# Masked attention and a two-layer MLP on one core: second-layer weights split ahead into DRAM, x work of GpSimd in halves, another order of the block products

## The chip, the cores and the metric

The kernel runs on one core of a Trainium2 chip. The metric is the device time of one execution in microseconds; less is better. A core has TensorE (PE, matrix products into PSUM), VectorE (DVE), ScalarE (ACT), GpSimd (POOL) and SyncE (SP, which here issues all the DMAs). Each engine works through its own queue in order; semaphores tie the queues together.

## The reference

Everything is float32, except that the weights come as 64-bit floats.

```python
scores = scale * q @ k.T                                  # 8 batches x 8 heads, 576 x 64
scores = where(scores >= max(scores) - tau, scores, -1e9)
attn = softmax(scores)
x = (attn @ v) arranged as (8 * 576, 8 * 64)              # 4608 tokens x 512
h = x @ w_in                                              # 512 -> 2048
g = maximum(h, 0) + alpha * minimum(h, 0)
out = g @ w_out                                           # 2048 -> 512
```

To keep float32's precision at a faster matmul, an operand is split in two parts of the type fp32r: hi is a rounded copy (always ACT, `split_hi`), lo is the original less hi (DVE or POOL, `split_lo`). A product then takes three matmuls: hi by hi, hi by lo, lo by hi.

## The kernel before

**Attention.** 32 pairs of heads, nine steps ("cycles") each, 288 in all. In cycle i DVE masks unit i, PE makes the scores of unit i+2 and turns unit i, and ACT makes the exponentials. What a pair needs behind its last unit (its products with v, the reciprocals, a trip of them through DRAM, three operations on POOL, the write of x to DRAM as `xs`) is queued some nine to seventeen cycles behind the pair's first unit. Into the gaps `Mlp.cycle` (line 759) puts work of the MLP for the first 6 of the 16 blocks of 128 hidden units: first-layer steps (`step_l1`, 12 matmuls for 256 tokens) and second-layer steps (`step_l2`). Tokens go in 18 groups of 256, and a group is ready when its batch's attention is done: groups 13 and 14 from cycle 265, and 15 to 17 only behind the last pair.

**Bridge.** What is left of these 18 groups becomes `jobs` (line 1028): for each, x is fetched (`fetch_x`), the first layer is made for six blocks, and the second layer of the job before (`second_layer`, 36 matmuls) stands behind the first of them. Beside it the first-layer weights of the other ten blocks are read from DRAM, where they were put, decoded, during the attention (`wid`); the seven sums that the next stage needs are made and split (`sums_at`) into the tiles `wa`.

**Stage A.** The remaining ten hidden blocks use a block scheme with seven products in place of eight (Winograd's form of Strassen's). Tokens go in six x blocks of 768; with the five pairs of hidden blocks that gives 30 units. `x_at` loads an x block, makes four sums (`sub7`, `add6`, `sub4`, `sub5`) and splits seven operands (hi on ACT, lo on POOL). `product_a` makes one product, six matmuls of 384 columns, per cycle. Products 1, 6, 5 and 3 of a unit add up in one PSUM bank X, 7 and 4 in W, 2 in Y; between two of a bank `after_a`, one cycle behind each product, reads the bank (ACT copies it to `c`, or DVE adds to it), and the bank's next product waits for that. `ORDER` is the order in which the products of neighbouring units follow each other. The results go to DRAM as `gd`. Meanwhile the second layer's weights are decoded from their 64-bit form, a block of 128 at a time, in steps on ACT, POOL and DVE (`word_at`: size, clamp, shift, sign, power, rest, done, a cycle apart) into the tile `wo32`. In the last five units `weights_b` makes the seven sums of each pair from it and splits them into the places of the first-layer weights as these fall free.

**Stage B.** The second layer of the ten blocks in the same scheme, nine units of seven products, 30 matmuls each. `gates_at` loads `gd` (as `gr`) and splits; `after_b` adds to the earlier partial sums (`pin`) and writes the output.

**What sets the order.** `at_cycle(c, fn)` puts a function into cycle c; all cycles are emitted in order, so PE, ACT, DVE and POOL run their instructions in this order, each as early as its data and its queue allow. The DMAs on SP are put in order by the framework.

Of the kernel before, what the change touches and what calls it, by code (L numbers as in the profile page):

```python
# [21 lines left out]
P = 128  # L22
# [3 lines left out]
F1 = 6  # L26
# [10 lines left out]
GB = 11  # L37
ENG1 = ('vpp', 'vpp')
# [42 lines left out]
def tile_masked_attention_moe(  # L81
# [606 lines left out]
    class Mlp:  # L688
# [70 lines left out]
        def cycle(self, i, used, slot):  # L759

            self.room = min(self.room, TH3) + CYCLE - used
            l1 = False
            if self.l1 and i >= self.gap and self.live < GB:
                if self.l1[0][2] is None:
                    self.step_l1(i)
                elif slot and self.room > TH1 and ("i", fcs1[self.l1[0][2]]) in ready:
                    l1 = True
                    self.room -= 1.31
            while self.l2 and self.l2[0][0] <= i and self.l2[0][4] in self.l2[0][2]["g"] and ("o", fcs1[self.l2[0][4]]) in ready and self.room > TH2:
                self.step_l2(i)  # L770
                self.room -= 0.216
            return l1
# [48 lines left out]
    ORDER = ((0, 1), (1, 5), (0, 7), (0, 2), (1, 3), (0, 6), (0, 4))  # L821
# [17 lines left out]
    def word_at(c, w, load, done, fc=None):  # L839


        def rest():
            low = f(w.low)
            w.eng[1].tensor_tensor(low, low, f(w.high), op=ALU.mult)

        at_cycle(load, w.load)
        at_cycle(c, w.size, *(() if fc is None else (tiny_sb[:, fc : fc + 1],)))
        at_cycle(c + 1, w.clamp)
        at_cycle(c + 2, w.shift)
        at_cycle(c + 3, w.sign)  # L850
        at_cycle(c + 4, w.power)
        at_cycle(c + 5, rest)
        at_cycle(c + 6, done, w)
# [48 lines left out]
    with tc.manual_schedule(engines=ENGINES) if ENGINES else ExitStack():  # L902
# [57 lines left out]
        left = [ExitStack() for _ in range(6)]  # L960
# [87 lines left out]
        first_weights(i + 4, 6)  # L1048
# [12 lines left out]
        def first_layer(job, j):  # L1061
            fc = fcs1[j]
            name = f"{job.name}_{fc}"
            while "x" not in job.x:
                cycle()
            ph = ps_2.tile([P, 512], F32, tag="ph", name=f"ph{name}", bufs=4)
            layer1_into(ph, fc, job.n, job.x["x"])
            cycle()
            t = prelu(mem.mp1, G1, fc, job.n, ph, name, 2)
            job.g[j] = mem.mp1.tile([P, 2, G1], F32R, tag="g", name=f"g{name}", bufs=GB)  # L1070
            split_g(job.g[j], t, job.n)
# [23 lines left out]
        for num, job in enumerate(jobs):  # L1095
            fetch(num + 1)
            for k, j in enumerate(job.todo):
# [7 lines left out]

        puts = second_layer(pending, mem.ws)
        left[2].close()
        p1.close()
        mem.xr = pool(2, "xraw", "left")
        mem.br = pool(3, "br", "right")  # L1110
        mem.pa = pool(4, "pa", "right")

        start = {}
        steps = []
        c = i + 1
        for n in range(NA + NB + 1):
            for lag, prod in {NA: TURN, NA + NB - 1: LAST, NA + NB: ()}.get(n, ORDER):
                u = n - lag
                if 0 <= u < NA + NB:
                    start[u, prod] = c  # L1120
                    steps.append((u, prod))
                    c += 1 if u < NA else 3
        begin = start[0, 1]
        end = c
        place = {step: n for n, step in enumerate(step for step in steps if step[0] >= NA)}
# [3 lines left out]
        def x_at(s):  # L1129
            u = s * NP  # L1130
            st = {}
            need = {n: start[u, n] for n in USE}
            first = s == 0

# [12 lines left out]
            tt = (nc.vector if first else nc.gpsimd).tensor_tensor  # L1147
# [20 lines left out]
            def hi(n):  # L1168
                slot = (7 * s + USE.index(n) - 7 * (NA // NP - 1)) % XB
                home = mem.pa if slot < 7 else mem.xr  # L1170
# [5 lines left out]
            def lo(n):  # L1176
                split_lo(nc.vector if first and n in (7, 6) else nc.gpsimd, xop[s, n][1], st[src(n)], xop[s, n][0])

            if first:
                at = lambda c, fn, *a: fn(*a)  # L1180
            else:
                at = at_cycle
            at(need[1] - 32, load)
            for m, n in enumerate(USE):
                c = need[1] - 22 + 3 * m
                if not first and m >= XB - 7:
                    c = max(c, start[u - 1, USE[m + 7 - XB]] + 2)
                fn = {7: sub7, 6: add6, 4: sub4, 5: sub5}.get(n)
                if fn:
                    at(c - 1, fn)  # L1190
                at(c, hi, n)
                at(c + 1, lo, n)

        x_at(0)
        for put in puts:
            put()
        left[5].close()
# [66 lines left out]
        wo32 = mem.br.tile([P, NP, 2, DM], F32, name="wo32")  # L1264
        def late_word(n, c):
            fc = fcs2[n]
            w = Split64(mem.ws, ("w0", 3), mem.ws, ("w1", 2), "ppp", *src_o(fc))

            def done(w):
                dst = wo32[:, n // 2, n % 2]  # L1270
                nc.vector.scalar_tensor_tensor(
                    dst, f(w.t), turn_sb[:, fc : fc + 1], f(w.low), op0=ALU.mult, op1=ALU.add
                )

            word_at(c, w, c - 4, done, fc)

        for n in range(NJ):
            late_word(n, begin + 8 + 14 * n)
# [3 lines left out]
        def weights_b(pr):  # L1282
            m = DM // 2
            u = NA - NP + pr
            blk = lambda j, k: wo32[:, pr, j, k * m : (k + 1) * m]
            st = {1: blk(0, 0), 2: blk(1, 0), 3: blk(1, 1), 5: blk(0, 1), 6: blk(0, 0), 4: blk(1, 0)}
            tt = nc.vector.tensor_tensor

            def sub7():
                st[7] = mem.br.tile([P, m], F32, tag="wt", name=f"wt{pr}", bufs=2)  # L1290
                tt(st[7], st[3], st[5], op=ALU.subtract)

            def sub5():
                tt(st[5], st[5], st[1], op=ALU.subtract)

            def add6():
                tt(st[6], st[7], st[1], op=ALU.add)

            def sub4():
                tt(st[4], st[2], st[6], op=ALU.subtract)  # L1300

            def hi(n):
                bsum[pr, n] = mem.wa.tile([P, 2, m], F32R, tag=f"wa{pr}_{n}", name=f"wb{pr}_{n}")
                split_hi(bsum[pr, n][:, 0], st[n])

            def lo(n):
                split_lo(nc.vector if n in (1, 2, 5) else nc.gpsimd, bsum[pr, n][:, 1], st[n], bsum[pr, n][:, 0])

            for n in USE:
                c = start[u, n] + 2  # L1310
                if n == 7:
                    at_cycle(c - 1, sub7)
                    at_cycle(c - 1, sub5)
                fn = {6: add6, 4: sub4}.get(n)
                if fn:
                    at_cycle(c, fn)
                at_cycle(c, hi, n)
                at_cycle(c + 1, lo, n)

        def gates_at(s):  # L1320
# [57 lines left out]
            for n in USE:  # L1378
# [4 lines left out]
                if fn:  # L1383
                    at_cycle(c - 2, fn)
# [32 lines left out]
        def turn_over():  # L1417
            left[2].close()
# [80 lines left out]
```

## Time and profile before

| | us |
|---|---|
| median of 3 runs | 1441.19 (1441.01 to 1441.2) |
| the profiled execution | 1439.3 |
| its span, from the first to the last instruction | 1437.5 |
| PE busy in the span | 1323.2 (92%) |
| DVE busy | 1143.2 (80%) |
| ACT busy | 971.8 (68%) |
| POOL busy | 745.6 (52%) |

The profile is of one execution. Its times count from the span's start. A row of a timeline has start, duration, engine, line, operation, out<-in, a count, and in brackets how long the engine sat idle before and who ended that. A group of instructions has its count, busy time and mean in ns, and the idle time before them. Matmuls are pipelined: two overlap, so their starts and not their durations give the pace, and a busy PE can still run at a lower granted clock.

### The profile page before, as it was taken

What the parts mean: (1) busy time and instruction counts of PE and PEld (TensorE: products, weight loads), DVE (VectorE), ACT (ScalarE), POOL (GpSimd) and SP (SyncE); (2) the same over time, 40 slices, a digit from 0 to 9 for tenths busy, and PEclk for the clock granted to TensorE, in tenths of its full rate; (3) what the DMA queues carried; (4) which work ended last, traced back from release to release, by engine and by line L of the source; (5) the groups of instructions that cost most, each with busy time, mean ns of one, the idle gap of its engine ahead of it and who ended that gap; (6) DMA issues with size and microseconds to landing.
All of it is one profiled execution on the core that took longest, in us unless ns stands there. A gap on an engine that the chain in (4) does not pass through costs nothing.

```text
span 1437.5 us, 26187 instructions
## 1 busy us (share of the span) xinstructions
PE 1323.2 (92%) x8998; PEld 1229.8 (86%) x8998; DVE 1143.2 (80%) x2122; ACT 971.8 (68%) x2109; POOL 745.6 (52%) x875
## 2 busy tenths in 40 slices
PE   5998999999899898999999998879888898999998
PEld 4666889989889898898889987778788898999998
DVE  7998988988978988888888855756666568878886
ACT  7887888888878887888888844356555565333332
POOL 4874765774765766666666646555465542000000
PEclk9999999999999999999999999989999999999999
DMA  7646455555545455455544314345452365656541
GB/s 227 187 115 171 126 138 143 156 151 145 157 127 146 138 150 149 132 158 146 144 136 131 85 48 156 103 146 157 154 161 94 127 202 174 195 180 205 190 144 59
DMA packets 146165, 210.31 MB, mean 146 GB/s; under 512 B 16016, under 2 KB 89008, under 8 KB 146032
## 3 DMA queue, kind: packets, MB, share of 16 engines
q1 hardware_dynamic: 146032, 208.63, 49.4%
q8 instruction: 72, 1.18, 0.3%
q14 instruction: 61, 0.50, 0.1%
HBM read 111.75 MB, written 54.67 MB: 116 GB/s over the span
## 4 chain that ended last, share of the span: by engine, by line
PE 59%; issue 11%; DVE 11%; ACT 8%; POOL 7%; DMA 3%; SPq 1%; POOLq 0%; DVEq 0%; ACTq 0%
PE av L577 10%; PE pX L1396 9%; PE s L430 9%; PE acca L253 7%; PE t L474 5%; PE pha L217 5%; PE pW L1396 4%; PE pX L1219 4%; PE pY L1396 2%; DVE p L465 2%; DVE nmx L445 2%; PE pW L1219 1%; POOL xl L869 1%; ACT p L453 1%; DVE eo L530 1%
## 5 line engine op out<-in xcount | busy, mean ns | idle before, releaser
L445 DVE TENSOR_REDUCE nmx<-s 128x1 f32<-128x576 f32 x288 | 216.7, 752 | 64.6 <-PE s L430 61.2
L465 DVE SCALAR_TENSOR_TENSOR p<-s,thr,p 128x576 f32<-128x576 f32 x256 | 206.8, 808 | 3.2 <-ACT thr L458 2.7
L453 ACT ACTIVATE p<-s,nmx 128x576 f32<-128x576 f32 x256 | 190.3, 743 | 8.8 <-DVE nmx L445 8.4
L430 PE MATMUL s<-kh,qst 128*128 128x288 f32 x640 | 144.9, 316 | 49.2 <-DVE p L465 31.7
L1219 PE MATMUL pX<-xh,wa 128*128 128x384 f32 x480 | 142.5, 355 | 43.3 <-DVE pZ L1259 25.4
L253 PE MATMUL acca<-wo,ga 128*128 128x512 f32 x540 | 168.8, 425 | 1.5 <-POOL ga L247 1.5
L430 PEld LDWEIGHTS s<-kh,qst 128*128 128x128 f32 x640 | 100.2, 192 | 79.4 <-issue 39.6
L474 PE MATMUL t<-ident,p 128*128 128x128 f32 x1024 | 156.5, 276 | 0.0
L217 PE MATMUL pha<-xh,wi 128*128 128x256 f32 x720 | 146.9, 287 | 6.1 <-ACT pra L230 4.6
L1219 PEld LDWEIGHTS pX<-xh,wa 128*128 128x128 f32 x480 | 92.7, 198 | 50.2 <-DVE pZ L1259 28.9
L430 PE MATMUL s<-kl,qst 128*128 128x288 f32 x640 | 133.9, 299 | 0.0
L1396 PE MATMUL pX<-wb,gh 128*128 128x256 f32 x720 | 130.2, 283 | 0.0
L217 PEld LDWEIGHTS pha<-xh,wi 128*128 128x128 f32 x720 | 117.4, 190 | 13.1 <-ACT pra L230 7.7
L474 PEld LDWEIGHTS t<-ident,p 128*128 128x128 f32 x1024 | 127.7, 143 | 0.2
L866 ACT ACTIVATE gh<-gr 128x1280 fp32r<-128x1280 f32 x45 | 57.4, 1276 | 88.2 <-PE pX L1396 39.2
L1396 PEld LDWEIGHTS pX<-wb,gh 128*128 128x128 f32 x720 | 112.2, 191 | 0.0
L577 PE MATMUL av<-eo,vst 128*128 128x322 f32 (+1 forms) x512 | 107.7, 334 | 0.2 <-ACT xb L590 0.2
L253 PEld LDWEIGHTS acca<-wo,ga 128*128 128x128 f32 x540 | 95.7, 194 | 14.0 <-POOL ga L247 1.9
L530 DVE TENSOR_TENSOR eo<-t,eo 128x512 fp32r<-128x512 f32 (+1 forms) x168 | 97.3, 592 | 9.8 <-ACT eo L526 9.3
L430 PEld LDWEIGHTS s<-kl,qst 128*128 128x128 f32 x640 | 102.6, 192 | 0.0
L1396 PE MATMUL pX<-wb,gl 128*128 128x256 f32 x360 | 101.7, 283 | 0.0
L217 PE MATMUL pha<-xl,wi 128*128 128x256 f32 x360 | 101.4, 282 | 0.0
(207 smaller groups left out, 3824.5 us busy)
## 6 DMA issues: line engine op xcount, KB each, us to landing
gd<-c SPq DMA_DIRECT2D x90, 192.0 KB
gr<-gd SPq DMA_DIRECT2D x24, 640.0 KB
kr<-in_k_dram SPq DMA_DIRECT2D x31, 320.0 KB
rb<-rvd SPq DMA_DIRECT2D x64, 144.0 KB
xs<-xa SPq DMA_DIRECT2D x32, 288.0 KB
pin<-part SPq DMA_DIRECT2D x18, 512.0 KB
out_dram<-pin SPq DMA_DIRECT2D x18, 512.0 KB
vr<-in_v_dram SPq DMA_DIRECT2D x28, 320.0 KB
```

The source lines that it names most:

```text
L217: nc.tensor.matmul(ph[:, :n], w[:, c, :], xx[:, c, :n], start=(c == 0 and ti == 0), stop=(c == NCC - 1 and ti == 2),)
L253: nc.tensor.matmul(acc[:m, :], gg[:, g, o : o + m], w, start=(first and ti == 0), stop=(last and ti == 2))
L430: nc.tensor.matmul(ps[:, h, :288], w, kk[:, a + h * 288 : a + (h + 1) * 288], start=(ki == 0 and i == 0), stop=(ki == 1 and i == n - 1),)
L445: nc.vector.tensor_reduce(self.nmx[:, j : j + 1], self.S[u][0][:, :, :288], axis=AX.XY, op=ALU.max, negate=True)
L453: nc.scalar.activation(pj, ps[:, :, :288], AF.Exp, bias=nmx[:, j : j + 1], scale=1.0)
L465: nc.vector.scalar_tensor_tensor(pj, ps[:, :, :288], thr[:, j : j + 1], pj, op0=ALU.is_ge, op1=ALU.mult, accum_out=self.sm[:, c : c + 1])
L474: nc.tensor.transpose(tb[:, c, :], pt[:, j, j * D + c * P : j * D + (c + 1) * P], ident)
L530: nc.vector.tensor_tensor(dst[1], ps, f(dst[0]), op=ALU.subtract)
L577: nc.tensor.matmul(pa[:m, :n], w, x, start=(part == 0 and c == 0), stop=(part == z.parts[-1] and c == NKC))
L866: nc.scalar.activation(dst, src, AF.Copy)
L1219: nc.tensor.matmul(ph[:, :H1], a, x[:, c], start=(fresh and c == 0 and ti == 0), stop=(c == 1 and ti == 2), skip_group_check=not fresh,)
L1396: nc.tensor.matmul(acc[:, tb * H2 : (tb + 1) * H2], g[:, pr, tb * P : (tb + 1) * P], w, start=(fresh and n == 0 and ti == 0), stop=(n == l ...
```

## The change

It has these parts. The diff has line numbers of the kernel before.

1. `HOLD = 14`: `Mlp.cycle` issues no first-layer step from cycle 274 on.
2. `ORDER` swaps its fifth and sixth entries: product 6 comes before the earlier unit's product 3.
3. `word_at` gets a pace. The second layer's words use `LATE`: size at 0, clamp 1, shift 3, sign 4, power 5, rest 6, done 9.
4. `late_pair` takes the place of `late_word` and `weights_b`: two words are decoded 12 cycles apart, their sums made, all seven split (lo always on POOL) and written to DRAM (`wod`), a pair every 28 cycles. `weights_b` only reads them back, two cycles behind the last use of the place.
5. From the second x block on, `x_at`'s sums and lo parts go to POOL as two instructions of 128x384 in place of one of 128x768.
6. The first x block is loaded, and its first operand made, ahead of the last two second layers of the bridge, which now follow each other; the rest of its operands comes behind them. For that three places of operands lie in a pool of their own (`xe`), and the last job's sixth g has a place in `ws`.
7. The first weights are 9 cycles apart in place of 6, and the gates' `sub3` has another cycle.

```diff
+HOLD = 14
...
-                elif slot and self.room > TH1 and ("i", fcs1[self.l1[0][2]]) in ready:
+                elif slot and i < total - HOLD and self.room > TH1 and ("i", fcs1[self.l1[0][2]]) in ready:
...
-    ORDER = ((0, 1), (1, 5), (0, 7), (0, 2), (1, 3), (0, 6), (0, 4))
+    ORDER = ((0, 1), (1, 5), (0, 7), (0, 2), (0, 6), (1, 3), (0, 4))
...
+    EARLY, LATE = (0, 1, 2, 3, 4, 5, 6), (0, 1, 3, 4, 5, 6, 9)
...
+        for d, step in zip(pace[1:], (w.clamp, w.shift, w.sign, w.power, rest)):
+            at_cycle(c + d, step)
+        at_cycle(c + pace[6], done, w)
...
-        first_weights(i + 4, 6)
+        first_weights(i + 4, 9)
...
             for k, j in enumerate(job.todo):
                 first_layer(job, j)
-                if k == 0 and pending:
+                if k == 0 and pending and not last:
                     second_layer(pending, mem.mp1)
-            pending = job
-        puts = second_layer(pending, mem.ws)
+            if not last:
+                pending = job
...
+            def tt(out, a, b, op):
+                if first:
+                    nc.vector.tensor_tensor(out, a, b, op=op)
+                else:
+                    for c in range(2):
+                        nc.gpsimd.tensor_tensor(out[:, c], a[:, c], b[:, c], op=op)
...
+            def lo(n):
+                xh, xl = xop[s, n]
+                if first and n in (7, 6, 2):
+                    split_lo(nc.vector, xl, st[src(n)], xh)
+                else:
+                    for c in range(2):
+                        split_lo(nc.gpsimd, xl[:, c], st[src(n)][:, c], xh[:, c])
+
+            if first:
+                for fn in (load, sub7):
+                    fn()
+                hi(1)
+                lo(1)
+                add6()
+                sub5()
+
+                def others():
+                    for n in USE[1:]:
+                        if n == 4:
+                            sub4()
+                        hi(n)
+                        lo(n)
+
+                return others
...
         left[2].close()
+        mem.xr = pool(2, "xraw", "left")
+        others = x_at(0)
+        second_layer(pending, mem.mp1)
+        puts = second_layer(jobs[-1], mem.ws)
         p1.close()
-        mem.xr = pool(2, "xraw", "left")
+        mem.xe = pool(6, "xe", "left")
         mem.br = pool(3, "br", "right")
         mem.pa = pool(4, "pa", "right")
+        others()
+        for put in puts:
+            put()
...
+        H = DM // 2
+        wod = [dram.tile([len(USE), P, 2, H], F32, name=f"wod{pr}") for pr in range(NP)]
+
+        def late_pair(pr, c):
+            st = {}
+
+            def done(r, w):
+                if r == 0:
+                    st["w"] = mem.br.tile([P, 2, DM], F32, tag="wq", name=f"wq{pr}", bufs=2)
+                fc = fcs2[2 * pr + r]
                 nc.vector.scalar_tensor_tensor(
-                    dst, f(w.t), turn_sb[:, fc : fc + 1], f(w.low), op0=ALU.mult, op1=ALU.add
+                    st["w"][:, r], f(w.t), turn_sb[:, fc : fc + 1], f(w.low), op0=ALU.mult, op1=ALU.add
                 )
...
+            def hi(n):
+                st["hl", n] = mem.br.tile([P, 2, H], F32R, tag="wb", name=f"wb{pr}_{n}", bufs=2)
+                split_hi(st["hl", n][:, 0], st[n])
+
+            def lo(n):
+                t = st["hl", n]
+                split_lo(nc.gpsimd, t[:, 1], st[n], t[:, 0])
+                nc.sync.dma_start(wod[pr][USE.index(n)], f(t))
+
+            for r in range(2):
+                fc = fcs2[2 * pr + r]
+                w = Split64(mem.ws, ("w0", 3), mem.ws, ("w1", 2), "ppp", *src_o(fc))
+                word_at(c + 12 * r, w, c + 12 * r - 8, lambda w, r=r: done(r, w), fc, LATE)
+            at_cycle(c + 24, sums)
+            for k, n in enumerate(USE):
+                at_cycle(c + 26 + 2 * k, hi, n)
+                at_cycle(c + 27 + 2 * k, lo, n)
+
+        for pr in range(NP):
+            late_pair(pr, begin + 8 + 28 * pr)
...
-            for n in USE:
-                c = start[u, n] + 2
...
+            def load(n):
+                bsum[pr, n] = mem.wa.tile([P, 2, H], F32R, tag=f"wa{pr}_{n}", name=f"wb{pr}_{n}")
+                nc.sync.dma_start(f(bsum[pr, n]), wod[pr][USE.index(n)])
+
+            for n in USE:
+                at_cycle(start[NA - NP + pr, n] + 2, load, n)
...
-                    at_cycle(c - 2, fn)
+                    at_cycle(max(need[6], need[2]) - 4 if n == 3 else c - 2, fn)
```

More of the change, by code (lines that the diff above doesn't have):

```diff
@@ L837, in tile_masked_attention_moe, with word_at @@
     wid = [dram.tile([P, DM], F32, name=f"wid{fc}") for fc in fcs2]
-    def word_at(c, w, load, done, fc=None):
+    EARLY, LATE = (0, 1, 2, 3, 4, 5, 6), (0, 1, 3, 4, 5, 6, 9)
+    def word_at(c, w, load, done, fc=None, pace=EARLY):
         def rest():
@@ L959, in tile_masked_attention_moe @@
         at.close()
-        left = [ExitStack() for _ in range(6)]
+        left = [ExitStack() for _ in range(7)]
         pool = lambda k, name, side: left[k].enter_context(tc.tile_pool(name=name, bufs=1, side=side, reuse_waits="tile"))
@@ L1096, in tile_masked_attention_moe @@
             fetch(num + 1)
+            last = num == len(jobs) - 1
             for k, j in enumerate(job.todo):
                 first_layer(job, j)
-                if k == 0 and pending:
+                if k == 0 and pending and not last:
                     second_layer(pending, mem.mp1)
-            pending = job
-        puts = second_layer(pending, mem.ws)
-        left[2].close()
-        p1.close()
-        mem.xr = pool(2, "xraw", "left")
[L1110 to L1125, printed above, removed]
+            if not last:
+                pending = job
         xop = {}
@@ L1131, in x_at @@
             st = {}
-            need = {n: start[u, n] for n in USE}
             first = s == 0
+            need = None if first else {n: start[u, n] for n in USE}
             def load():
@@ L1189, in x_at @@
                 if fn:
[L1190 to L1194, printed above, removed]
+                    at_cycle(c - 1, fn)
+                at_cycle(c, hi, n)
+                at_cycle(c + 1, lo, n)
+        left[2].close()
+        mem.xr = pool(2, "xraw", "left")
+        others = x_at(0)
+        second_layer(pending, mem.mp1)
+        puts = second_layer(jobs[-1], mem.ws)
+        p1.close()
+        mem.xe = pool(6, "xe", "left")
+        mem.br = pool(3, "br", "right")
+        mem.pa = pool(4, "pa", "right")
+        others()
         for put in puts:
             put()
+        start = {}
+        steps = []
+        c = i + 1
+        for n in range(NA + NB + 1):
+            for lag, prod in {NA: TURN, NA + NB - 1: LAST, NA + NB: ()}.get(n, ORDER):
+                u = n - lag
+                if 0 <= u < NA + NB:
+                    start[u, prod] = c
+                    steps.append((u, prod))
+                    c += 1 if u < NA else 3
+        begin = start[0, 1]
+        end = c
+        place = {step: n for n, step in enumerate(step for step in steps if step[0] >= NA)}
         left[5].close()
@@ L1271, in done, with sums @@
                 nc.vector.scalar_tensor_tensor(
-                    dst, f(w.t), turn_sb[:, fc : fc + 1], f(w.low), op0=ALU.mult, op1=ALU.add
+                    st["w"][:, r], f(w.t), turn_sb[:, fc : fc + 1], f(w.low), op0=ALU.mult, op1=ALU.add
                 )
-            word_at(c, w, c - 4, done, fc)
-        for n in range(NJ):
-            late_word(n, begin + 8 + 14 * n)
+            def sums():
+                blk = lambda j, k: st["w"][:, j, k * H : (k + 1) * H]
+                st.update({1: blk(0, 0), 2: blk(1, 0), 3: blk(1, 1), 5: blk(0, 1)})
+                for n in (7, 6, 4):
+                    st[n] = mem.br.tile([P, H], F32, tag=f"sumo{n}", name=f"sumo{n}_{pr}")
+                tt = nc.vector.tensor_tensor
+                tt(st[7], st[3], st[5], op=ALU.subtract)
+                tt(st[6], st[7], st[1], op=ALU.add)
+                tt(st[5], st[5], st[1], op=ALU.subtract)
+                tt(st[4], st[2], st[6], op=ALU.subtract)
@@ L1287, in weights_b @@
[L1287 to L1304, printed above, removed]
@@ L1417, in turn_over @@
         def turn_over():
+            left[6].close()
             left[2].close()
```

42 lines of the change are left out of this document (7 added, 35 removed).

## The prediction, made before the changed kernel had run

> **What bounds the kernel now.** I cut the span at the stages that the code has and read the windows view first. Columns: TensorE busy (instructions), its weight loads, DVE, ACT, POOL, then granted clock, DMA share and GB/s.
>
> ```profile
> 806.00:840.00 34.00, 34.00 (x251) 32.50 (x250) 30.15 (x68) 27.27 (x69) 18.27 (x23) 1.00 0.12 43
> 840.00:868.50 28.50, 25.78 (x152) 22.10 (x150) 7.48 (x17) 8.47 (x21) 11.69 (x17) 1.00 0.23 72
> 868.50:928.00 59.50, 54.05 (x325) 48.24 (x326) 39.12 (x73) 26.59 (x71) 40.89 (x51) 0.94 0.43 141
> 928.00:1206.00 278.00, 234.66 (x1256) 227.49 (x1255) 178.71 (x288) 156.71 (x304) 141.27 (x97) 0.95 0.44 143
> 1206.00:1437.50 231.50, 227.09 (x1897) 226.88 (x1895) 182.81 (x164) 79.90 (x67) 2.82 (x2) 0.99 0.53 169
> ```
>
> From 1206.0 (stage B, second layer) TensorE never waits and the change leaves its 1,890 matmuls alone: nothing to win there. From 928 to 1206 (stage A, first layer, 30 units of seven products) 43 us are idle. The same view for line 1219 alone, one row for each x block of five units, and last a stretch without a stall:
>
> ```profile
> 928.00:976.30 48.30, 38.02 (x198) 37.07 (x198) 0.89 0.42 135
> 976.30:1023.30 47.00, 40.15 (x212) 39.10 (x211) 0.93 0.44 140
> 1023.30:1069.10 45.80, 38.85 (x212) 37.90 (x211) 0.96 0.50 156
> 1069.10:1115.70 46.60, 39.87 (x211) 38.80 (x211) 0.93 0.36 119
> 1115.70:1157.50 41.80, 37.37 (x212) 36.41 (x211) 1.00 0.37 124
> 1157.50:1206.00 48.50, 40.39 (x217) 37.88 (x216) 0.98 0.55 179
> 1126.70:1144.40 17.70, 17.70 (x104) 17.70 (x103) 1.00 0.32 111
> ```
>
> The last row holds 17 products of six matmuls: 1.041 us each. Five units, 35 products, would take 36.4 us; the blocks take 41.8 to 47.0. The first row (33 products, 34.4 us) is 13.9 long, the next four together 35.6, the last (36 products to the first of stage B, 37.5 us) 11.0: **60.5 us lost in stage A**. The granted clock of 0.89 to 0.96 in the long rows is part of it: behind a long gap the matmuls run slower for a few us.
>
> Who ends the waits (waits view, 928 to 1206; us in total, times, longest):
>
> ```profile
> PE pX L1219 <- DVE pZ L1259: 25.4, 10, 5.4
> PE pX L1219 <- ACT c L1236: 17.9, 10, 6.4
> POOL xl L869 <- ACT xh L866: 76.7, 27, 12.3
> ```
>
> Products 1, 6, 5, 3 of a unit add into one bank X, and each must wait until ACT or DVE has read the one before. Those two are not full; they are held up. The timelines of the longest stall and of one that comes with every x block:
>
> ```profile
> 1001.58 2.03 POOL L1161 TENSOR_TENSOR xt<-xt,xr 128x768 f32<-128x768 f32 x1
> 1001.94 2.22 DVE L152 SCALAR_TENSOR_TENSOR wto<-wro,wto 128x512 int32<-128x512 int32 x1
> 1006.71 2.27 DVE L1271 SCALAR_TENSOR_TENSOR wo<-wto,turn_sb,wro 128x512 f32<-128x512 f32 x1 [0.62 <-POOL wro L844]
> 1010.10 0.69 PE L1219 MATMUL pX<-xh,wa 128*128 128x384 f32 x1 [5.42 <-DVE pZ L1259]
> 1022.72 1.58 ACT L866 ACTIVATE xh<-xr 128x768 fp32r<-128x768 f32 x2 [1.71 <-POOL xr L1158]
> 1025.67 0.44 PE L1219 MATMUL pX<-xh,wa 128*128 128x384 f32 x1 [1.14 <-ACT c L1236]
> ```
>
> A decode step on DVE that reads and writes SBUF stands still until GpSimd's whole x operation is over (2.22 and 2.27 us); the `done` step also waits for GpSimd's multiply. Behind them in DVE's queue is pZ, and TensorE loses 5.42. In the second kind ACT's hi copy waits for a GpSimd subtraction, and the copy that frees the bank is queued behind it.
>
> By the Trainium skill ("SBUF — State Buffer", Who interferes with whom) the shared port pair is an exclusive lock held for the whole instruction. The two DVE rows agree; by that rule an x operation cut in two bounds such a wait by its half.
>
> **The change part by part.** *Halves, equal gaps, later decode steps, weights ahead.* GpSimd's durations:
>
> ```profile
> L77 POOL TENSOR_TENSOR kl<-kr,kh 128x320 fp32r<-128x320 f32 x8 | 7.0, 894 | 21.4 <-ACT kh L357 21.4
> L1158 POOL TENSOR_TENSOR xr<-xr,xr 128x768 f32<-128x768 f32 x5 | 9.2, 1844 | 0.0
> L869 POOL TENSOR_TENSOR wb<-wo,wb 128x256 fp32r<-128x256 f32 x15 | 13.7, 913 | 20.5 <-ACT wb L866 17.6 <-PE pW L1219 2.9
> L844 POOL TENSOR_TENSOR wro<-wro 128x512 f32<-128x512 f32 x10 | 10.4, 1040 | 19.4 <-DVE wro L157 14.9 <-PE pW L1219 4.6
> L144 POOL TENSOR_SCALAR wto<-wto 128x512 f32<-128x512 f32 x10 | 6.2, 618 | 13.5 <-ACT wto L140 13.5
> ```
>
> Between 320 (0.894) and 768 elements (1.844) a 128x384 half is 1.03 us, so a pair costs 2.06 against 1.84: eleven pairs a block, +2.4 us of GpSimd. In exchange the longest block of a DVE step falls from some 1.85 to 1.03, twice or three times per word. 6 to 5 and 5 to 3 are four products apart instead of three: one product, 1.04 us, more slack at both kinds of stall; 1 to 6 falls from five to four, where no stall stood. `done` comes three cycles behind the multiply instead of one, so its wait goes. Against this GpSimd gets all 35 subtractions of the split second layer (0.74 to 0.91 each; 20 before) and gets them between units 5 and 23, beside the x work. Per block of 35 cycles: 22 halves 22.7, 2.5 words 2.5 x (0.62+1.04) = 4.1, 8.75 subtractions x 0.85 = 7.4: **34.2 us of 36.4**. That leaves hardly room for its waits (76.7 us over five blocks now, most of it slack), so TensorE will be held to GpSimd's pace where a pair's subtractions meet x work. The 41.3 us of losses in the blocks (35.6 and 5.7 of the first row, at the third unit) fall, I estimate: the steady stalls of 1.1 to 1.3 stay at about 1 in five blocks, 5 us; the decode stalls all but go, 3 us; the new meetings cost 2 to 3 us in four blocks, 10 us. I take 18 left, **-23 us**; bounds 8 left (-33) and all 41 left (0).
>
> *DRAM.* 35 tiles of 256 KB are written (9.2 MB over 150 us, 60 GB/s beside a share of 0.36 to 0.50: hidden; but SP waits at each for POOL's subtraction, and the `c` writes queue behind it: part of the 10 us above), and read back in the last five units, each when its first-layer twin has been used.
>
> ```profile
> 1170.00:1180.00 10.00, 9.54 (x54) 8.94 (x53) 8.15 (x19) 5.90 (x15) 3.26 (x4) 1.00 1.03 353
> gd<-c SPq DMA_DIRECT2D x90, 192.0 KB
> ```
>
> 353 GB/s at a share of 1.03 is the ceiling here. Until the first product of stage B can start, 27 of the tiles (21 of pairs 0 to 2, five of pair 3, one of pair 4) must land (7.1 MB), beside 17 writes of 192 KB (3.3), four gate loads of 640 KB (2.6) and two of 512 KB (1.0): 14.0 MB, 40 us at 353 against 37.5 us of products, and a landing on top. That queue also holds the writes of `c` (two buffers, and ACT waits for them). The wb work that leaves ACT, DVE and POOL there frees part of the 11.0 lost. I take 13.5 left, **+2.5 us**; bounds -6 and +12.
>
> *x early.* At 928 three products ran and then
>
> ```profile
> 938.00 0.69 PE L1219 MATMUL pX<-xh,wa 128*128 128x384 f32 x1 [6.42 <-ACT c L1236]
> ```
>
> because the copy stood behind six hi copies that waited for x. Now x is loaded, and the operands of product 1 made, under 72 second-layer matmuls (16.7 us); those of 2, 6, 4, 5 need memory that the last second layer frees, so ACT still has about 4 us of copies near the start. Of the 8.2 us lost there (13.9 less 5.7) 1.5 stay: **-6.7 us**; bounds -8 and -3.
>
> *HOLD.* No first-layer step is issued in the attention's last 14 cycles and after. Counts from 806 to 868.4 (first row) and from 829 (second), then the end of the attention:
>
> ```profile
> L217 PE MATMUL pha<-xh,wi x72: 277/283/386, 807.4 to 857.2; 128*128 128x256 f32 x72
> L253 PE MATMUL acca<-wo,ga x74: 387/389/499, 829.8 to 867.1; 128*128 128x512 f32 x74
> 840.03 0.81 DVE L465 SCALAR_TENSOR_TENSOR p<-s,thr,p 128x576 f32<-128x576 f32 x1
> 864.48 0.38 SPq L637 DMA_DIRECT2D xs<-xa  x1
> 874.02 0.58 PE L217 MATMUL phj<-xhj,wi 128*128 128x256 f32 x1 [3.47 <-ACT xhj L888]
> 912.86 7.12 PE phj L217 x60
> 908.27 4.59 PE accj L253 x19
> ```
>
> 72 is nine groups of eight: three of token group 13 and all six of group 14 go behind the attention (12 matmuls x 0.119 = 1.42 us each), and with them both groups' second layers (72 x 0.232 = 16.7): 29.5 us of TensorE work. Now that work covers the wait for the last head pair. Without it the last 11 cycles run at DVE's pace, 30.15 busy of 34: the last mask comes some 4 us earlier, at 836. The tail from it to the xs write takes 24.4 us now; where the stuffing between its matmuls is gone I count 16, so 852. From xs to steady first layers took 10 us (864.5 to 874.0). TensorE has only group 13's three steps (4.3 us) until then, since group 14's x is fetched behind the pair's write on SP and split behind its last operations on POOL. So first layers of group 14 run from 862; behind that lie 24 of them (34.1), ten half second layers (41.8): 938, against 928 now: +10. If SP takes the fetch ahead of the write, POOL still frees only at 852 and the start is near 856: +4. I take **+8 us**; bounds -6 (the bridge hides the 6.7 us of gaps at 861 to 875) and +12. The first weights nine cycles apart instead of six lie under the same work, and the gates' sub3 lies in stage B, where TensorE waits for nothing: 0.
>
> **Sum**: -23 + 2.5 - 6.7 + 8 = -19.2. The profiled run took 1439.3 us (span 1437.5), the median is 1441.2, 1.9 above; the difference is taken from the median: 1422.
>
> **Rivals.** (a) *The held work bridges* the end of the attention, as group 13's x is there: -6 in place of +8, 1408. For it: gaps and a clock of 0.94 stand just there. Against: nothing but three steps is ready. (b) *DMA binds the last block*: gate loads fill the queue ahead of the weights, ACT waits for `c`: +12 in place of +2.5, 1431. For it: the row at 353 GB/s. (c) *GpSimd becomes the bound of stage A*, slower than before: its busy 34.2 us a block plus waits. From 11.1 us of waits a block the blocks are as long as now (45.3 in the mean of the four rows). If it keeps the 76.7 / 5 = 15.3 us that it waits for ACT today, a block is 49.5: five times +4.2, with +2.5, -6.7 and +8 gives 1466; at 12 us of waits 1449, which I take. Against: today's waits are mostly waits for the next block. The Trainium skill ("GPSIMD Engine Reference", When to use GPSIMD) speaks for this rival: elementwise work on two inputs belongs on VectorE, GpSimd being about half as fast. The trace agrees, with 455 ns for the same subtraction on DVE against 913:
>
> ```profile
> L869 DVE TENSOR_TENSOR wb<-wo,wb 128x256 fp32r<-128x256 f32 x14 | 6.4, 455 | 0.0
> ```
>
> (d) *The equal gaps do little*, as the stalls only move to other products: 30 of 41 left, 1434.
>
> **How the numbers follow.** A difference under 0.2% (2.9 us) can't be told from none by measuring this kernel. Chances: forecast 0.47 (1412 to 1432), (a) 0.19 (1400 to 1414), (b) 0.13, (d) 0.08, (c) 0.13. Half of (d) and a tenth of (c) end within 0.2%: 0.05; slower has the rest of (c), 0.12; faster 0.83. The range leaves out (c) and the lowest of (a): 1402 to 1437.
>
> **What would show it.** Right: stall rows on pX fall from 43 to about 20 us, L152 and L1271 never over 1.8; the first product of stage A near 936 and no 6-us gap behind it; DMA at 1.0 share in the last five units; stage B as long as now. Wrong: first product at or before 928; POOL busy under 80% from 976 to 1150 with stalls left; blocks of 46 us.

## The result, and the profile after

The changed kernel took **1456.9 us** (median of four runs, 1454.1 to 1458.3), the kernel before 1441.1 on the same chip: a ratio of 1.011 (95% interval 1.0092 to 1.0127). It is 1.1% slower, where 1.3% faster was forecast, and outside the range. The profiled execution took 1454.1 us, its span 1452.3; the span before was 1437.5, so 14.8 us are to be found.

The windows view after, in the columns of the prediction. The cuts are those at which the same work begins, so the bridge now ends at 941.6 and stage A at 1220.6:

```profile
840.00:868.50 28.50, 13.73 (x72) 12.38 (x73) 8.82 (x19) 7.04 (x20) 13.03 (x18) 0.70 0.37 118
868.50:941.60 73.10, 73.10 (x455) 66.00 (x454) 40.57 (x79) 29.20 (x75) 42.26 (x54) 1.00 0.35 109
941.60:1220.60 279.00, 238.91 (x1256) 230.37 (x1255) 160.29 (x269) 154.19 (x305) 161.92 (x171) 0.94 0.60 198
1220.60:1452.30 231.70, 227.08 (x1897) 226.51 (x1895) 181.46 (x167) 80.03 (x66) 0.00 (x0) 1.00 0.56 179
```

Stage B is as long as before (231.7 and 231.5). Stage A takes 279.0 in place of 278.0: nothing was gained there. The bridge ends at 941.6 in place of 928.0, 13.6 us later; its first row has 72 matmuls where there were 152. The same view for the products alone (line 1249 is the former 1219), one row for each block of five units as before, and last the first five products:

```profile
941.60:986.60 45.00, 38.68 (x199) 38.04 (x199) 0.89 0.40 126
986.60:1032.60 46.00, 39.46 (x211) 37.86 (x210) 0.96 0.60 198
1032.60:1082.60 50.00, 41.21 (x213) 38.64 (x212) 0.93 0.54 179
1082.60:1131.60 49.00, 42.07 (x211) 40.47 (x210) 0.90 0.56 183
1131.60:1172.80 41.20, 37.45 (x213) 36.32 (x212) 1.00 0.50 170
1172.80:1220.60 47.80, 40.00 (x217) 38.85 (x216) 0.96 0.95 324
941.60:952.60 11.00, 7.29 (x30) 6.97 (x30) 0.74 0.38 120
```

Against the same steady lengths (34.4, four times 36.4, 37.5) these rows lose 10.6, 40.6 (9.6 + 13.6 + 12.6 + 4.8) and 10.3 us: 61.5, where 60.5 were lost before.

**The bridge.** The timeline from the last mask to the first product of a job:

```profile
837.65 0.81 DVE L466 SCALAR_TENSOR_TENSOR p<-s,thr,p 128x576 f32<-128x576 f32 x1
850.90 1.20 POOL L628 TENSOR_TENSOR xa<-xa,rb 128x576 f32<-128x576 f32 x1 [2.64 <-DMA rb<-rvd]
853.96 0.33 SPq L638 DMA_DIRECT2D xs<-xa  x1
855.30 1.85 SPq L881 DMA_DIRECT2D xrj<-xs  x4
861.47 0.58 PE L218 MATMUL phj<-xhj,wi 128*128 128x256 f32 x1 [11.19 <-ACT xhj L888]
```

The last mask comes 2.4 us sooner than before, and the last write of x to DRAM at 854.0 in place of 864.5, but between 850.3 and 861.5 TensorE has nothing: the three held steps of group 13 are done, and the next x is loaded only behind that write on SP's queue, and then split.

**Stage A.** Who ends the waits of TensorE and of ACT (waits view, 941 to 1221):

```profile
PE pX L1249 <- ACT c L1266: 25.9, 13, 3.7
PE pW L1249 <- ACT c L1266: 12.4, 6, 4.9
PE pX L1249 <- DVE pZ L1289: 1.7, 6, 0.4
...
ACT xh L866 <- POOL xt L1136: 27.8, 12, 3.9
ACT wb L866 <- DMA wod<-wb: 20.6, 11, 5.4
ACT xh L866 <- POOL xr L1136: 15.9, 5, 3.9
ACT c L1266 <- DMA gd<-c: 14.0, 2, 8.1
```

The waits for DVE's pZ, 25.4 us before, are all but gone (1.7). In their place stand waits for ACT's copies, on bank X 25.9 (17.9 before) and on bank W 12.4 (none before). ACT itself stands in its hi copies: 43.7 us (27.8 + 15.9) for GpSimd's x sums, 20.6 for the write of the split weights to DRAM. In the kernel before, its waits for the sums were 24.7 us:

```profile
ACT xh L866 <- POOL xr L1158: 10.7, 5, 2.4
ACT xh L866 <- POOL xt L1161: 8.6, 5, 2.5
ACT xh L866 <- POOL xt L1154: 5.4, 5, 1.4
```

Two stalls show how that reaches TensorE. One with a sum:

```profile
1014.02 2.63 POOL L869 TENSOR_TENSOR xl<-xr,xh 128x384 fp32r<-128x384 f32 x2
1016.62 1.97 POOL L1136 TENSOR_TENSOR xt<-xt,xr 128x384 f32<-128x384 f32 x2
1018.62 0.84 ACT L866 ACTIVATE xh<-xt 128x768 fp32r<-128x768 f32 x1 [3.52 <-POOL xt L1136]
1019.37 0.56 ACT L1266 ACTIVATE c<-pX,turn_sb 128x384 f32<-128x384 f32 x1
1019.99 0.45 PE L1249 MATMUL pX<-xh,wa 128*128 128x384 f32 x1 [1.95 <-ACT c L1266]
```

and one with a buffer:

```profile
1038.13 0.92 POOL L869 TENSOR_TENSOR wb<-wq,wb 128x256 fp32r<-128x256 f32 x1
1040.46 4.42 SPq L1327 DMA_DIRECT2D wod<-wb  x3
1043.32 0.42 ACT L866 ACTIVATE wb<-sumo 128x256 fp32r<-128x256 f32 x1 [5.37 <-DMA wod<-wb]
1043.64 0.56 ACT L1266 ACTIVATE c<-pW,turn_sb 128x384 f32<-128x384 f32 x1
1044.26 0.69 PE L1249 MATMUL pW<-xh,wa 128*128 128x384 f32 x1 [3.37 <-ACT c L1266]
```

In both, the copy that TensorE needs (line 1266) is ready to run and stands in ACT's queue behind a hi copy that waits. In the first that hi copy stands one cycle behind its sum, and the sum only starts when GpSimd has two halves of a lo part behind it. In the second it wants one of two buffers `wb`, and the tile before last has not landed: GpSimd was done with it at 1039.05, SP issued its write at 1040.46, and the buffer came free at 1043.32, 4.3 us later, some four cycles of a product.

### The profile page after: what moved, and what is told of

The parts are those of the page before. It is cut to its first block, busy times and chain, and to the rows that moved or that the text cites. A ratio compares the mean times of both kernels' runs of the same rounds, so it can differ in the third digit from the quotient of the medians.

```text
span 1452.3 us, 26445 instructions
## 1 busy us (share of the span) xinstructions
PE 1328.4 (91%) x8998; PEld 1234.0 (85%) x8998; DVE 1125.7 (78%) x2114; ACT 968.6 (67%) x2112; POOL 756.6 (52%) x939
## 4 chain that ended last, share of the span: by engine, by line
PE 60%; DVE 10%; ACT 9%; POOL 9%; issue 8%; DMA 4%; SPq 0%; POOLq 0%; ACTq 0%; DVEq 0%
PE av L578 10%; PE s L431 9%; PE pX L1427 9%; PE acca L254 6%; PE t L475 5%; PE pW L1427 4%; PE pha L218 4%; PE pX L1249 3%; POOL xl L869 3%; PE phj L218 2%; PE accj L254 2%; DVE p L466 2%; PE pY L1427 2%; DVE nmx L446 2%; POOL xt L1136 2%
## 5 line engine op out<-in xcount | busy, mean ns | idle before, releaser
L1249 PE MATMUL pX<-xh,wa 128*128 128x384 f32 x480 | 144.0, 357 | 28.0 <-ACT c L1266 25.9
L254 PE MATMUL acca<-wo,ga 128*128 128x512 f32 x468 | 149.5, 428 | 0.0
L218 PE MATMUL pha<-xh,wi 128*128 128x256 f32 x648 | 132.5, 288 | 5.9 <-ACT pra L231 4.3
L218 PEld LDWEIGHTS pha<-xh,wi 128*128 128x128 f32 x648 | 105.7, 190 | 12.3 <-ACT pra L231 7.0
L254 PEld LDWEIGHTS acca<-wo,ga 128*128 128x128 f32 x468 | 82.9, 195 | 10.0 <-DVE e L531 0.3
L218 PE MATMUL pha<-xl,wi 128*128 128x256 f32 x324 | 91.4, 282 | 0.0
```

Of the source, the lines that this page charges most:

```text
L218: nc.tensor.matmul(ph[:, :n], w[:, c, :], xx[:, c, :n], start=(c == 0 and ti == 0), stop=(c == NCC - 1 and ti == 2),)
L254: nc.tensor.matmul(acc[:m, :], gg[:, g, o : o + m], w, start=(first and ti == 0), stop=(last and ti == 2))
L1249: nc.tensor.matmul(ph[:, :H1], a, x[:, c], start=(fresh and c == 0 and ti == 0), stop=(c == 1 and ti == 2), skip_group_check=not fresh,)
```

## The experiments

All were timed beside the kernel before on the same chip; its medians there were 1441.7 to 1442.9. The 1456.9 of the changed kernel stands beside 1441.1, so differences to it are uncertain by up to 1.8 us from that alone. "Stage A" is the time from the first product of the first unit to the first of stage B in the profiled run (278.0 before, 279.0 after).

**The held steps, in part and whole.** `a_hold0`:

```diff
-HOLD = 14
+HOLD = 0
```

> The changed kernel, but the attention issues first-layer steps to its end again. Theory HOLD (the 11.2 us in which TensorE waits for the x of the last groups, and the 13.6 us by which stage A starts later, come from the held steps alone): the attention covers its tail again, first product at 927 to 930 in place of 941.6, time 1457 - 12 = 1443 to 1447. Rival (the later start comes from the reordered bridge, from the x of the first block ahead of the last two second layers and the first weights nine cycles apart): the first product stays at 938 or later, the time at 1453 or more.

1449.8 us (ratio 1.004, 1.0025 to 1.0056), first product at 934.3. The condition `i < total - HOLD` with 0 still refuses the steps of the cycles behind the attention's last, so this was half an undoing. `a_nohold` undoes all of it:

```diff
-HOLD = 14
+HOLD = -99
```

> The changed kernel with first-layer steps issued without a limit, as before (the run with HOLD = 0 still held those of the closing cycles behind the attention: 24 of its 60 matmuls went behind the last pair). Theory HOLD (all of the 13.6 us by which stage A starts later is the held work): the wait of 11 to 12 us for the x of the last groups goes, first product at 927 to 930, time 1443 to 1446. Rival (half of it comes from the two last second layers now standing together, from x ahead of them or from the weights nine cycles apart): first product at 933 or later, 1448 to 1452.

**1444.6 us** (1.0015, 0.9998 to 1.0033), first product at 927.6, where the kernel before has 928.0: the later start came from the held steps. The wait for the x of the last jobs is back to that of before:

```profile
PE phj L218 <- ACT xhj L888: 4.6, 2, 3.6
```

Stage A itself took 285.0 us in the profiled run, 6.0 more than in the changed kernel. Of these, 2.2 are new waits at its start, for the operands of product 7: their hi copy stands behind the hi copies of the first-layer weights, which keep ACT until 929.5. The rest wasn't taken apart, so the reordered bridge isn't cleared of a small cost.

Holding the steps cost 12.3 us of time (1456.9 - 1444.6). With it undone the changed kernel is about as fast as the one before: parts 2 to 7 together gained nothing.

**The order.** `a_order` goes back to the order of before:

```diff
-    ORDER = ((0, 1), (1, 5), (0, 7), (0, 2), (0, 6), (1, 3), (0, 4))
+    ORDER = ((0, 1), (1, 5), (0, 7), (0, 2), (1, 3), (0, 6), (0, 4))
```

> The changed kernel with the order of the products as before (product 6 behind the earlier unit's product 3). Theory ORDER (product 6 now comes four products behind product 1, and ACT's late copies stop it there): the waits for ACT's copy of bank X fall from 25.9 to about 15 us, but the waits for DVE's pZ return (2.0 to about 12): 1452 to 1458. If equal gaps are a loss altogether: below 1450. Rival (equal gaps help as forecast): 1465 or more.

1468.0 us, 11 more: the rival, equal gaps help. Waits for pZ come back, and those for ACT's copies of bank X do not fall:

```profile
PE pX L1249 <- ACT c L1266: 26.4, 12, 5.8
PE pX L1249 <- DVE pZ L1289: 15.0, 5, 4.1
```

So the order is not why TensorE waits for ACT, but it decides at which product. By the timelines, with the former order product 5 waits 21.1 us for the copy of product 6, and product 6 waits for the copy of product 1 only in the first unit (3.7). In the changed kernel product 5 waits 10.6 us, and product 6 15.2, of which 11.5 are behind the first unit.

**The buffers.** `a_buf4`:

```diff
-                st["hl", n] = mem.br.tile([P, 2, H], F32R, tag="wb", name=f"wb{pr}_{n}", bufs=2)
+                st["hl", n] = mem.br.tile([P, 2, H], F32R, tag="wb", name=f"wb{pr}_{n}", bufs=4)
```

> The changed kernel with four buffers for the split second-layer weights in place of two. Theory TWO BUFFERS (ACT stands 20.6 us in its hi copies until a DRAM write has landed, and the copies that free the banks stand behind it): those waits go to under 2 us, the blocks of 46 to 50 us fall by 2 to 3 each: 1445 to 1449. Rival (GpSimd's queue holds ACT: x sums behind subtractions and multiplies): ACT only waits for GpSimd instead, 1454 to 1458.

**1445.0 us**, 11.9 less; stage A 264.9. ACT's wait for the writes falls from 20.6 to 3.3 us, that for the sums stays:

```profile
ACT xh L866 <- POOL xt L1136: 30.9, 11, 4.1
ACT xh L866 <- POOL xr L1136: 15.1, 5, 3.8
...
ACT wb L866 <- DMA wod<-wb: 3.3, 1, 3.3
```

**Who subtracts.** `a_lodve` has the lo parts of the weights on DVE:

```diff
-                split_lo(nc.gpsimd, t[:, 1], st[n], t[:, 0])
+                split_lo(nc.vector, t[:, 1], st[n], t[:, 0])
```

> The changed kernel with the lo parts of the second layer's weights on DVE in place of GpSimd. Theory GPSIMD FULL (35 subtractions of 0.74 to 0.9 us in GpSimd's queue make the x sums late, and ACT waits 43.7 us for these): ACT's waits for the x sums fall by half, 1445 to 1449. Rival (two buffers: ACT waits for the DRAM writes whoever subtracts): 1453 to 1457.

1445.1 us, as the theory said, but not by its mechanism: ACT waits for the sums as long as before (27.0 + 15.3), and what fell is the wait for the writes (7.4 in place of 20.6). A likely reason is that a tile that DVE subtracts at once is also written sooner: one tile's hi copy began at 1036.98, its subtraction at 1037.43, its write at 1037.89. A time that comes out right didn't show the cause here; the waits did.

**Halves.** `a_whole`:

```diff
-                    for c in range(2):
-                        split_lo(nc.gpsimd, xl[:, c], st[src(n)][:, c], xh[:, c])
+                    split_lo(nc.gpsimd, xl, st[src(n)], xh)
```

and the sums likewise.

> The changed kernel with GpSimd's x operations of 128x768 in one instruction again. Theory HALVES HELP (a DVE decode step stands still for a half in place of a whole): the decode steps on DVE reach 2.2 us again and the waits for pZ return to 6 to 10 us, 1460 to 1466. Rival (halves only lengthen GpSimd's queue, by 2.4 us an x block, and ACT waits for the second half): ACT's waits for the x sums fall from 43.7 to about 35 us, 1450 to 1454. Neither: within 2 us of 1457.

1451.2 us: 5.8 less, the rival. The decode step on DVE does stand still longer again; these are its shortest, median and longest duration in ns, first with halves (the changed kernel), then whole:

```profile
L153 DVE SCALAR_TENSOR_TENSOR wto<-wro,wto x10: 681/683/973, 960.1 to 1129.7; 128x512 int32<-128x512 int32 x10
```

```profile
L153 DVE SCALAR_TENSOR_TENSOR wto<-wro,wto x10: 678/689/2328, 961.5 to 1126.6; 128x512 int32<-128x512 int32 x10
```

But ACT waits 6.0 us less for sums (23.8 + 13.9), and in this kernel ACT is what TensorE waits for: its waits for ACT's copies fall from 38.3 to 33.1 us, while those for pZ grow from 1.7 to 4.6.

**The distance of the sums.** `a_sum3`, for the x blocks from the second on:

```diff
                 if fn:
-                    at_cycle(c - 1, fn)
+                    at_cycle(c - 3, fn)
                 at_cycle(c, hi, n)
```

> The changed kernel with each x sum three cycles ahead of its hi copy in place of one. Theory SUMS TOO CLOSE (a sum in halves takes 2.0 to 2.4 us, more than a cycle of 1.04, so that ACT waits 43.7 us in its hi copies and the copies that free the banks are queued behind): those waits fall below 20 us, 1444 to 1450. Rival (GpSimd is late by its whole load there, wherever the sums stand in its queue): waits and time as in the changed kernel, 1454 to 1458.

**1438.4 us**: 18.5 less, more than expected, and by this one line the changed kernel passes the one before (0.9976, 0.9962 to 0.9989). Stage A takes 262.3. ACT's waits for the sums all but go (the longest left is 1.2 us), those for the buffers grow, and bank X loses half of its wait:

```profile
PE pX L1249 <- ACT c L1266: 13.6, 7, 3.7
PE pW L1249 <- ACT c L1266: 13.1, 6, 4.9
...
ACT wb L866 <- DMA wod<-wb: 29.5, 14, 5.3
...
ACT xh L866 <- POOL xt L1136: 3.3, 4, 1.2
```

**The three together.** `c_best` has `HOLD = -99`, four buffers and the sums three cycles ahead.

> The changed kernel with three edits together: first-layer steps without a limit, four buffers for the split weights, x sums three cycles ahead. If the three costs are separate (13.6 for the held steps, 12 for the two buffers as measured, 6 to 10 for the sums): 1421 to 1427, faster than the kernel before by 1%. If buffers and sums are the same loss (ACT held up) and only one counts: 1430 to 1433.

**1411.0 us**, ratio **0.9796** (0.9769 to 0.9824), and 45.9 us less than the changed kernel, where the three edits alone gave 12.3, 11.9 and 18.5, together 42.7. By the ratios, each to the kernel before beside it, the three give 3.3% and the kernel with all of them 3.1%. So they add up, as separate costs do, within the spread (the expectation had put the sums at 6 to 10). Stage A takes 251.2, with GpSimd a little busier than in the changed kernel (167.9 us, 161.9 there):

```profile
925.60:1176.80 251.20, 229.70 (x1256) 224.00 (x1255) 175.18 (x277) 157.24 (x314) 167.87 (x175) 0.96 0.68 225
```

**On this kernel, the other parts once more.** `c_whole` has whole x operations, by the edit of `a_whole`:

> The kernel of three edits (1411) with GpSimd's x operations in one instruction again. Theory HALVES COST AT THE SUMS ONLY (with the sums three cycles ahead ACT no longer waits for a second half, and what is left is the shorter stand-still of DVE's decode steps): whole operations are slower, 1414 to 1420. Rival (a half pair is 2.0 to 2.4 us of GpSimd against 1.84, and GpSimd's time counts everywhere): whole operations gain as they did in the changed kernel (5.8), 1404 to 1408.

1416.3 us: 5.2 more. With the sums early, halves help; pZ's wait is 10.9 us in place of 6.0. `c_early` has the decode steps a cycle apart:

```diff
-                word_at(c + 12 * r, w, c + 12 * r - 8, lambda w, r=r: done(r, w), fc, LATE)
+                word_at(c + 12 * r, w, c + 12 * r - 8, lambda w, r=r: done(r, w), fc, EARLY)
```

> The kernel of three edits (1411) with the decode steps of the second layer a cycle apart again (pace 0 1 2 3 4 5 6). Theory LATER STEPS HELP (done then waits on DVE for GpSimd's multiply, and pZ is queued behind it): DVE's waits at done rise from 1.5 to 8 us or more, 1415 to 1421. Rival (with the rest in order the multiply comes in time anyway): 1409 to 1413.

1421.8 us: 10.8 more. `done` waits for GpSimd's multiply again, and pZ behind it:

```profile
PE pX L1249 <- DVE pZ L1289: 16.7, 9, 3.4
...
DVE wq L1305 <- POOL wro L847: 12.9, 8, 2.4
```

`c_spread` makes the first x block's operands 4, 5 and 3 within stage A, with the lo part of 4 on DVE:

```diff
-        others()
+        others((7, 2, 6))
...
+        for d, n in ((2, 4), (4, 5), (6, 3)):
+            at_cycle(begin + d, others, (n,))
```

> The kernel of three edits (1411), with the first x block's operands 4, 5 and 3 split in the cycles in which stage A already runs, in place of all six at once behind the bridge, and the lo part of 4 on DVE. Theory QUEUE AT THE START (the copies of banks X and W stand behind six hi copies on ACT, first five products 14.5 us in place of 5.2): these fall to 8 to 10 us, time 1405 to 1408. Rival (TensorE there waits for the memory that the last second layer frees, and for the first weights, wherever the copies stand): 1410 to 1413.

1413.3 us, a miss: the stall at the start falls (from 3.87 to 0.78 us), as the theory said, but a new one of 2.75 us, behind ACT's copy again, stands at 961, and the time is not better.

`c_c76` gives the results c of products 7 and 6 a third buffer:

```diff
-                t = sv[u, prod] = mem.br.tile([P, H1], F32, tag=f"c{prod}", name=f"c{prod}_{u}", bufs=2)
+                t = sv[u, prod] = mem.br.tile([P, H1], F32, tag=f"c{prod}", name=f"c{prod}_{u}", bufs=2 if prod == 1 else 3)
```

> The kernel of three edits (1411) with three buffers in place of two for the results c of products 7 and 6, which ACT copies from the banks. Theory BUFFERS (in the last five units ACT waits 16.0 us for writes of c that stand behind the weights' read-back, and TensorE twice for ACT, 1.8 and 5.0 us; with a third buffer there is time for the write to land): these waits fall below 5 us, last block 46.2 to about 41, time 1405 to 1408. Rival (the queue at its 353 GB/s is the bound, and the wait comes back at the gates of stage B or at the next buffer): last block 45 or more, 1409 to 1413.

**1407.5 us** (0.9758, 0.9738 to 0.9779), the fastest of all. The last five units, first in `c_best` and then here:

```profile
1130.60:1176.80 46.20, 39.37 (x218) 38.73 (x217) 22.61 (x37) 18.17 (x36) 1.71 (x2) 0.96 0.98 335
```

```profile
1134.30:1176.10 41.80, 39.62 (x219) 38.98 (x218) 22.62 (x38) 18.03 (x36) 1.78 (x2) 0.96 1.00 344
```

The queue is as full in both; 4.4 us go because ACT needn't wait for a write that stands behind others: its waits for the writes of c fall from 16.0 to 8.3 us, and TensorE's for ACT's copies of bank W from 6.8 to 0.2. So about half of what this block loses in `c_best` (46.2 against the steady 37.5) was a matter of buffers; whether the rate is the bound of the rest wasn't tried. The gain of 3.5 us in the medians is less sure than that of the block: the 95% intervals of the two kernels just overlap, and the two profiled runs differ by 0.6 us only, as stage A, 6.6 us shorter here (244.6), also starts 5.8 us later, behind code that the edit leaves alone.

**On the kernel before.** `b_halves` (the halves alone, the edit of part 5) and `b_sum3` (the edit of `a_sum3` alone):

> The kernel before with one edit: GpSimd's x sums and lo parts from the second x block on in two instructions of 128x384. As the prediction had it (a DVE decode step stands still for a half in place of a whole): waits for pZ fall from 25.4 to 15 us or less, 1434 to 1438. Rival (ACT's hi copies wait for the second half of a sum that stands one cycle ahead, and the bank copies behind them): 1443 to 1448.

1441.7 us, ratio 0.9999 (0.9987 to 1.001): neither. TensorE's wait for pZ falls a little (25.4 to 22.7). ACT's waits for GpSimd's sums grow from 24.7 to 32.0 (20.4 + 11.6), and TensorE's for ACT's copies from 17.9 to 19.5; together TensorE's two waits are nearly what they were.

> The kernel before with one edit: each x sum from the second x block on stands three cycles ahead of its hi copy in place of one. Theory SUMS TOO CLOSE ALREADY BEFORE (ACT waited 24.7 us for GpSimd's sums, each x block had its stall behind that): ACT's waits for GpSimd fall below 8 us, time 1432 to 1437. Rival (this loss came only with the halves and the weights in GpSimd's queue; before, pZ on DVE is the stall): 1439 to 1443.

**1425.0 us**, ratio 0.9889 (0.9861 to 0.9917): better than the theory asked for. The sums too close to their copies were a loss already in the kernel before: two cycles earlier are worth 17.4 us (1442.3 on that chip). ACT's waits for GpSimd's sums, 24.7 us before, are no longer in the view at all, the wait for ACT's copies of bank X falls from 17.9 to 11.9 us and that for pZ from 25.4 to 20.8.

## Why the prediction was wrong, step by step

The 14.8 us of the span by the prediction's own steps, with the lost times of the rows above:

| step | forecast | measured |
|---|---|---|
| halves, gaps, decode steps, weights ahead | -23 | +4.1 (41.3 lost before; 40.6 + 4.8 after) |
| DRAM read-back, last five units | +2.5 | -0.7 (11.0 before, 10.3 after) |
| x early | -6.7 | -2.4 (8.2 before, 5.8 after) |
| HOLD | +8 | +13.6 (928.0 to 941.6) |
| stage B | 0 | +0.2 |

The rows set two profiled runs side by side. The start of stage A varies by some us from run to run: it lies between 939.6 and 943.9 in the six kernels with `HOLD = 14`, and between 924.6 and 931.4 in the six with -99. Writing the weights ahead, and x early, were not undone singly.

**The step that failed is the -23**: it left 18 us of losses, and 45.4 stayed. It was worked out of three pieces, 5 us of steady stalls, 3 of decode stalls and 10 of new meetings. The piece on DVE was right: the longest decode steps, at most 1.8 us by forecast, took 0.97 (L153) and 1.48 (`done`), and the waits for pZ all but vanished. The load of GpSimd was right too: 34.2 us a block by forecast, 33.3 to 35.1 measured in the three long ones.

The steady stalls were mis-sized. They are the prediction's second kind, a hi copy on ACT that waits for a GpSimd sum with the bank's copy queued behind it, and they were put at 5 us. The sum stands one cycle, 1.04 us, ahead of its hi copy; a whole sum took 1.84 us, one in halves takes 2.0 to 2.3, behind more GpSimd work. So ACT's waits for sums grew from 24.7 to 43.7 us. `a_sum3` takes 18.5 us off the changed kernel, and `b_sum3` 17.4 off the kernel before: the greater part of this loss was there already, and the change did nothing for it.

The new meetings were taken for GpSimd's pace, to which TensorE would be held. It wasn't: `c_best` has the same GpSimd work and blocks of 37.8 to 41.9 us. The sign that the prediction itself had named came up: from 986.6 to 1131.6 GpSimd is busy 71%, under the 80% named, in blocks of 46 to 50 us.

One wait had no price. The hi copies of the weights wait for DRAM writes with only two buffers: the prediction followed the write on SP, and called the transfer hidden, but left out who waits for the buffer (20.6 us; freed by `a_buf4`, -11.9). The sentence "1 to 6 falls from five to four, where no stall stood" failed as well: behind the first unit product 6 waited for nothing before, and in the change it waits 11.5 us; the first stall shown is one of these. Stalls were counted as gone where their cause on DVE went, while the other releaser of the same bank grew later.

Three parts within the step have the signs that it gave them: the order is worth 11 us in the change itself (`a_order`), and once ACT is freed the later decode steps are worth 10.8 (`c_early`) and the halves 5.2 (`c_whole`). In the change the halves cost 5.8 (`a_whole`), where ACT waits 6.0 us more for the longer sums. The Trainium skill ("Perfetto Trace Analysis", Optimizing Scalar/DVE Operations) says that where ScalarE and VectorE aren't full but hold up other engines, breaking up their instructions may let work be done sooner. Here GpSimd's instructions were broken up: that gained nothing on the kernel before, cost 5.8 us in the change and gained 5.2 in `c_best`, so in these runs it depends on who waits for the second half. By the Trainium skill's lock rule ("SBUF — State Buffer", Who interferes with whom) a half bounds DVE's stand-still. The traces agree: the longest L153 takes 2.33 us with whole operations, 0.97 with halves here and 1.45 at most in the other runs with halves, where one undisturbed takes 0.68 and a half 1.0 to 1.2.

Stage A in `c_best` (251.2) lies near what the forecast for its parts gave (278.0 - 27.2 = 250.8), but that is no proof of them: `b_sum3` reaches 264.2 with none of the change, so only the other 13 us can be the change's, with four buffers.

**HOLD: the mechanism was right and its size too small.** The events came where they were put: the last mask at 837.65 (836 by forecast), the write of x at 854 (852), three steps of group 13 and then nothing, the first layer of the next job at 861.5 (862). From there the held work was to take 75.9 us, to 938, and took 80.1, to 941.6. Of the 4.2 us more, 2.6 are a wait for the lo parts of x that the working left out, just behind the first matmul: on GpSimd these stand behind three lo parts of first-layer weights (861.25 to 863.7). The prediction put the new spacing of these weights at 0; whether the spacing does it no run shows. Matmuls that run slow behind the gap (a clock of 0.50 from 861.4 to 868.5) are part of the rest, which wasn't taken apart. And the term was set at 8, though its own working gave 10, because the start might come sooner; it didn't. Of the bounds (-6 and +12) the upper was too low by 1.6. Rival (a), held work as a bridge, is refuted.

**x early** kept 5.8 of 8.2 us in place of 1.5. Product 6 still waits for a copy that stands behind the hi copies of 2, 6, 4, 5 and 3. These start only at 941.18, as the last second layer ends; the profile names no releaser, and by the code they need memory which that layer frees:

```profile
941.18 0.85 ACT L866 ACTIVATE xh<-xr 128x768 fp32r<-128x768 f32 x1 [6.18 <-issue]
...
948.60 0.69 PE L1249 MATMUL pX<-xh,wa 128*128 128x384 f32 x1 [3.68 <-ACT c L1266]
```

The prediction named those "4 us of copies" and then let only 1.5 stay.

**DRAM** was right within its bounds. The queue is full (a share of 1.04 from 1190 to 1200 at 353 GB/s, 1.05 in the next 10 us at 398, so 353 was not its ceiling), and rival (b)'s wait is there (ACT for writes of c, 1.9 us before, 14.0 after). Something gave as much back; the weights' work that left those units is the likely part, but no run shows it. Rival (c), slower, had the sign but not the cause. Rival (d), that stalls move to other products, is nearest to what happened in stage A; it was given 0.08, and at 30 left it was still too hopeful.

## What to carry to other kernels

Before counting a stall as gone, list every engine that must release the same buffer or bank, and follow in each one's queue what stands ahead of the releasing instruction: an engine that is 55% busy can still be the bound when a copy waits behind something that waits. Put a producer on a slow engine as far ahead of its in-order consumer as its duration asks (here three cycles and not one, 17 us for one line), and give a tile that is written to DRAM buffers for the whole time until the write has landed. A time that comes out as expected doesn't show the mechanism; the waits view does.

## What the runs showed that was not expected

A 256 KB tile in SBUF was free again 4.3 us after its last part was made, 1.4 us of them before SP issued the write and 2.9 behind that, at a DMA share of 0.89 in these 2.9 us (0.54 in the whole block). Two buffers for a tile every two products (2.1 us) are not enough for that.
